# Six separate PSUM banks for the mixing products, weight sums loaded in pieces, and small transfers issued by ScalarE: one change to a fused attention and token-mixing kernel

## The chip, the cores and the metric

The kernel runs on one core of a Trainium2 chip. A core has TensorE (matrix products into PSUM), VectorE, ScalarE and GpSimd (elementwise work), SyncE (which here does nothing but issue transfers) and 16 DMA engines. In the profile they are PE and PEld (matmul and weight load of TensorE), DVE, ACT, POOL and SP. The metric is the device time of one launch in microseconds (us); lower is better.

## What is computed

```python
# attention, per batch and head: only keys of the query's own cluster count
mask = q_assign[:, :, :, None] == k_assign[:, :, None, :]
scores = np.where(mask, scale * np.matmul(q, k.transpose(0, 1, 3, 2)), -1e9)
x = softmax(scores) @ v                      # then laid out as (4, 768, 512)
# token mixing
theta = x @ w_theta
zr, zi = x * np.cos(theta), x * np.sin(theta)
y = np.einsum('ts,bsd->btd', w_tok_r, zr) + np.einsum('ts,bsd->btd', w_tok_i, zi)
u = x + y
out = u + np.maximum(u @ w_ch, 0.0)
```

There are 4 batches of 768 tokens and 512 channels (8 heads of 64). Everything is float32. On TensorE a float32 operand is split into a high and a low part in a shorter float format, and a product is the sum of high by high, high by low and low by high: three matmuls instead of one.

## The kernel before

**Two phases.** The attention of all 16 head pairs comes first (until about 450 us); it writes x to DRAM. The change leaves its code alone. The token mixing of the four batches follows. A batch has six tiles of 128 tokens, numbered n = 6 b + t.

**Per tile: theta.** `theta_parts` (L930) loads the tile's columns of x (`xs`, `load_columns`, L919), splits them (`xh` by ScalarE, L935; `xl` by VectorE in the first two batches, by GpSimd in the last two, L937). `rotation_angle` (L655) makes 12 matmuls into one bank `tp`. `rotation_reduce` (L662) reduces the angle in three VectorE steps (L666 to L668) and takes its absolute value on ScalarE (L670). `rotation_turn` (L651) transposes the tile x on VectorE (`xn` from `xb`, L652) and then issues the next tile's `xb` as four transfers of 64 KB (`load_blocks`, L638, L647); there is one `xb` buffer. Then ScalarE takes two sines (L964; L985 in the first two batches) and VectorE multiplies them by `xn` (L971; L987).

**Batches 0 and 1 ("plain").** `mix` (L1017) multiplies the split tile by the split weights, 48 matmuls, accumulating over the six tiles in six PSUM banks. All six banks are one tile, `y` (L849). After the sixth tile `channel_plain` (L1173) adds y to x (`add_y`, L1152), splits the sum (L1154, L1155) and makes eight groups of 12 matmuls with `w_ch` (L1162), two of them in other banks, six in banks of `y`; `channel_out` (L1166) takes each group out by one VectorE instruction (`ot`, L1169) and one transfer. The order of this stretch is made by a planner that runs the program on a cost model and puts each engine's instructions in the order in which they become ready there.

**Sums of weights.** For batches 2 and 3 the two-by-two block product (cosine and sine parts by the two weights' halves) is made from seven products of sums, as in Strassen's scheme. `make_forms` (L1047) makes the seven split sums of each of six tiles (42 in all: a VectorE sum L1061, a ScalarE cast L1062, a GpSimd subtraction L1063, a store of 384 KB). It is a generator; the plain loop advances it by five steps after each `mix` but the first and the last (L1207). `load_forms` (L1067) loads one tile's seven sums, 384 KB each.

**Batches 2 and 3.** Here the order on each engine, SyncE too, is the program's order (`in_order`, L689). `mix_forms` (L1105) makes 21 matmuls per tile and half of the channels: product m = 4 goes into a bank of its own, `four`, the other six into the six banks of `y`. The first half goes over tiles 0 to 5 while theta of later tiles is worked on, the second half back over 5 to 0. At the end of a half `add_products` (L1116) adds the seven products to x in twelve additions: three instructions of 768 columns for products 4, 3 and 1, and in its second part two of 768 columns that read two banks at once and two of 384. `split_z` (L1079) makes the sums and splits of the rotated tile for the next `mix_forms`; the half of the rotated tile that the second half needs is stored to DRAM (`zd`, L977) and loaded again (`zb`, `load_z`, L1073). `channel` (L1181) starts five groups with the first half's channels and goes on with the second half's.

The sums of tile 4 lie in the buffers `u` of the channel product, those of tile 5 in the place of tile 0's, so neither stays resident: tile 4's seven are loaded between the channel product of one batch and the next batch (L1245, L1295), tile 5's after tile 0's `mix_forms` (L1257), tile 0's again after the second half's tile 5 (L1276). x of the next batch (`load_x`, 1.5 MB) is issued behind the channel product (L1294). All transfers are issued by SyncE, one queue, in order.

Of the kernel before, what the change touches and what calls it, by code (L numbers as in the profile page):

```python
# [9 lines left out]
F32 = mybir.dt.float32  # L10
# [4 lines left out]
ALU = mybir.AluOpType  # L15
AX = mybir.AxisListType
PSUM = bass.MemoryType.PSUM
# [24 lines left out]
def kernel(  # L42
# [19 lines left out]
    nc = tc.nc  # L62
    B, H, D, S = qT.shape
    P = 128
    NP = H // 2
    NT = S // P
    C = cent.shape[0] // H
    DM = w_theta.shape[0]
    NCT = DM // P
    HS = S // 2  # L70
# [4 lines left out]
    xT_d = [dram.tile([P, NP, S], F32, name=f"xT_d{b}") for b in range(B)]  # L75
# [116 lines left out]
    for x in range(3):  # L192
        x = (NPAIR + x) % 3
# [67 lines left out]
    def f(ap):  # L261
        return ap.bitcast(F32)
# [60 lines left out]
    def turn_one_hot(pi, n):  # L323
        ot = bank(f"ot{pi}{n}").bitcast(BF16)[:, 0:S]
        for t in range(NT):
            nc.tensor.transpose(
                out=ot[:, t * P:(t + 1) * P], in_=ohp[:, n, t].rearrange("p j c -> p (j c)"), identity=identb)
        return ot
# [267 lines left out]
    def run(gen):  # L596
        for _ in gen:
            pass
# [39 lines left out]
    def load_blocks(n):  # L638
        if n == B * NT:
            return  # L640
        b, t = divmod(n, NT)
        xb = blocks[n] = ma[0].tile([P, DM], F32, tag="xb", name=f"xb{n}")


        for a in range(P // 32):
            src = xT_d[b][:, :, t * P + 32 * a:t * P + 32 * a + 32]
            nc.sync.dma_start(  # L647
                out=xb[32 * a:32 * a + 32].rearrange("c (n m r) -> c n m r", n=NP, m=P // 32),
                in_=src.rearrange("(m c) n r -> c n m r", c=32))

# [144 lines left out]
    while u <= NUT or todo:  # L795
# [8 lines left out]
        if 0 <= u < NUT:  # L804
            both(score_products, u, exps)
            if u == 0:
# [4 lines left out]
                for n, x in ((1, "mk"), (0, "mq")):  # L811
                    nc.scalar.activation(
                        out=st[1][x], in_=turn_one_hot(1, n), func=AF.Identity,
# [31 lines left out]
    def mpool(name, bufs=1, **kw):  # L845
        return mctx.enter_context(tc.tile_pool(name=name, bufs=bufs, **kw))

    pm = [mpool("pm0", space=PSUM)]
    y = mpool("py", space=PSUM).tile([P, 6, 512], F32, name="y")  # L849
    pm.append(mpool("pm1", space=PSUM))  # L850
    mx = mpool("mx")
    ma.append(mpool("ma1"))
# [12 lines left out]
    def mbank(name):  # L865
        banks[0] += 1
        return pm[(banks[0] - 1) % 2].tile([P, 512], F32, tag="bank", name=name)
# [10 lines left out]
    def load_x(b):  # L878
        xT = xts[b] = mx.tile([P, NP, S], F32, tag="xT", name=f"xT{b}")
        if b == 0:  # L880

            for p in range(NP):
                nc.sync.dma_start(out=xT[:, p], in_=xT_d[b][:, p])
        else:
            nc.sync.dma_start(out=xT, in_=xT_d[b])
# [31 lines left out]
    columns = {}  # L917

    def load_columns(n):  # L919

        b, t = divmod(n, NT)
        if 0 < b < B:
            columns[n] = mxs.tile([P, NCT, P], F32, tag="xs", name=f"xs{n}")
            with tc.issue_after(last_load[0].ins):
                nc.sync.dma_start(out=columns[n], in_=xT_d[b][:, :, t * P:(t + 1) * P])

    PLAIN = 2
    turning = {}
# [31 lines left out]
    z_d = {}  # L960
# [13 lines left out]
    def keep_turned(b, t, rab):  # L974
        zs[b, t] = rab
        z_d[b, t] = dram.tile([P, 2, DM // 2], F32, tag=f"z{t}", name=f"zd{b}_{t}", bufs=2)
        nc.sync.dma_start(out=z_d[b, t], in_=rab[:, :, DM // 2:DM])  # L977

    def rotate(b, t, rab, xn):
        if b < PLAIN:  # L980
# [21 lines left out]

    def y_at(d, c0, c1):
        bank, c = divmod(d * S + c0, 512)
        return y[:, bank, c:c + c1 - c0]

    def cuts(d, c0=0, c1=S):

# [24 lines left out]
    ORDER = (4, 3, 1, 5, 2, 6, 7)  # L1033
    Z_AT = {5: 0, 2: 1, 1: 2, 3: 3, 6: 4, 7: 5, 4: 6}
    Y_AT = {3: 0, 1: 1, 5: 2, 2: 3, 6: 4, 7: 5}
# [28 lines left out]
                nc.sync.dma_start(out=w_f[t][:, m - 1], in_=f(to))  # L1064
                yield

    def load_forms(t):  # L1067
        for m in ORDER:
            nc.sync.dma_start(out=f(forms[t][m]), in_=w_f[t][:, m - 1])

    second = {}
# [28 lines left out]
    four = {}  # L1100

    def product(m):
        return four[0][:, 0:HS] if m == 4 else y[:, Y_AT[m], 0:HS]

    def mix_forms(tiles, first, last):  # L1105

# [9 lines left out]
    def add_products(b, h, k):  # L1116

        x = xts[b][:, 2 * h:2 * h + 2].rearrange("p d (l n) -> p (d l) n", l=2)

        def add(to, of, op):  # L1120
            nc.vector.tensor_tensor(out=to, in0=to, in1=of, op=op)  # L1121

        def twice(m):
            return product(m).unsqueeze(1).broadcast_to([P, 2, HS])

        if k == 0:
            add(x[:, 0:3:2], twice(4), ALU.add)
            add(x[:, 1:4:2], twice(3), ALU.subtract)
            add(x[:, 0:4:3], twice(1), ALU.add)
        else:  # L1130
            add(x[:, 0:4:3], y[:, 2:4, 0:HS], ALU.subtract)
            add(x[:, 1:3], y[:, 2:4, 0:HS], ALU.add)
            add(x[:, 3], product(6), ALU.add)
            add(x[:, 0], product(7), ALU.subtract)

    def split_u_part(b, h, us, eng):

# [7 lines left out]
    def add_y(b, c0, c1):  # L1145

        xT, n = xts[b], c1 - c0
        uh, ul = (u_tile(f"u{x}{b}_{c0}")[:, :, 0:n] for x in "hl")
        for d in range(NCT):
            x = xT[:, d, c0:c1]  # L1150
            for n0, n1, _ in cuts(d, c0, c1):
                nc.vector.tensor_tensor(  # L1152
                    out=xT[:, d, n0:n1], in0=y_at(d, n0, n1), in1=xT[:, d, n0:n1], op=ALU.add)
            nc.scalar.copy(out=uh[:, d, :], in_=x)  # L1154
            nc.gpsimd.tensor_tensor(out=ul[:, d, :], in0=x, in1=f(uh[:, d, :]), op=ALU.subtract)  # L1155
        return uh, ul

    def channel_products(cp, e, u, ds):
        uh, ul = u
        for k, (uu, w) in enumerate(((uh, 0), (uh, 1), (ul, 0))):  # L1160
            for d in ds:
                nc.tensor.matmul(  # L1162
                    cp, lhsT=w_c[d][w][:, e * P:(e + 1) * P], rhs=uu[:, d, :],
                    start=k == 0 and d == 0, stop=k == 2 and d == NCT - 1, skip_group_check=True)
# [8 lines left out]
    def channel_plain(b):  # L1173
        us = [add_y(b, ch * HS, (ch + 1) * HS) for ch in range(2)]
        for x in range(2 * NCT):
            ch, e = divmod(x, NCT)
            cp = (mbank(f"cp{b}_{x}") if x < 2 else y[:, x - 2])[:, 0:HS]
            channel_products(cp, e, us[ch], range(NCT))
            channel_out(b, e, ch, cp)

# [19 lines left out]
    for n in range(PLAIN * NT):  # L1200
        b, t = divmod(n, NT)
        theta(*divmod(n + AHEAD, NT))
        if b == 0:
            weights_after[0] = splits[n + 1]
            next(late_weights, None)
        mix(b, t)
        if 0 < n < PLAIN * NT - 1:  # L1207
            for _ in range(5):
                next(new_forms, None)
        if n == PLAIN * NT - 2:  # L1210
            run(new_forms)
            load_forms(0)
            load_forms(1)
        if t == NT - 1:
            if b == PLAIN - 1:
                load_forms(2)
                load_forms(3)
            channel_plain(b)
            load_x(b + 1)
# [8 lines left out]
    def before(n):  # L1228
        if n < last:
            theta_parts(n, nc.gpsimd)  # L1230
# [10 lines left out]
    def done(n):  # L1241
        if n in turning:
            turned(n)

    load_forms(4)  # L1245
    before(PLAIN * NT + 2)
    z = split_z(PLAIN, 0, 0)
    for b in range(PLAIN, B):
        for t in range(NT - 1):
            n = b * NT + t  # L1250
            done(n + 1)
            angle(n + 2)
            before(n + 3)
            now, z = z, split_z(b, t + 1, 0)
            mix_forms([(t, now)], t == 0, False)
            if t == 0:
                load_forms(5)  # L1257
            turn(n + 2)
            if t == NT - 2:
                load_z(b, 5)  # L1260
        n = b * NT + NT - 1
        load_z(b, 4)
        done(n + 1)
        now, z = z, split_z(b, 5, 1)
        load_z(b, 3)
        mix_forms([(5, now)], False, True)
        angle(n + 2)
        add_products(b, 0, 0)
        now, z = z, split_z(b, 4, 1)
        load_z(b, 2)  # L1270
        add_products(b, 0, 1)
        before(n + 3)
        for t in (5, 4, 3, 2, 1, 0):
            mix_forms([(t, now)], t == 5, t == 0)
            if t == 5:
                load_forms(0)  # L1276
            if t > 1:
                now, z = z, split_z(b, t - 2, 1)
                load_z(b, t - 4)
            else:  # L1280
                now = z
            if t == 5:
                turn(n + 2)
            if t == 4:
                done(n + 2)
                split_u_part(b, 0, us, nc.vector)
        for k in range(2):
            add_products(b, 1, k)
        split_u_part(b, 1, us, nc.vector)
        if b + 1 < B:  # L1290
            z = split_z(b + 1, 0, 0)
        channel(b, us)
        if b + 1 < B:
            load_x(b + 1)  # L1294
            load_forms(4)  # L1295
    in_order(begin)
    mctx.close()

# [50 lines left out]
```

## Time and profile before

| | |
|---|---|
| median of three runs | 886.58 us (885.67 to 886.92) |
| the profiled execution | 885.21 us |
| its span, first to last instruction | 883.4 us |
| TensorE busy | 788.0 us (89%) |
| VectorE, GpSimd, ScalarE busy | 640.4, 563.6, 415.3 us |
| transfers | 135.37 MB, 47.9% of 16 DMA engines |

The durations in the rows below are those of the profiled execution; 1.8 us of its time lie outside the span. A row of the timeline gives the start, the length, engine, line, operation, output and inputs and their shapes, a count, and in brackets the idle time of that engine just before it and what ended that. A row of the waits gives the waiting engine and line, what it waited for, the total in us, the number of times and the longest. A row of the chain gives start, length and what it was. A row of the windows gives from and to, the length, the busy time and number of instructions of each engine, the granted TensorE clock, and the busy share and GB/s of the DMA engines.

### The profile page before, as it was taken

Reading aid. Unit: us, or ns where it says so; the run is one execution under the profiler, and the core shown is the slowest. Engines: PE = TensorE matmul, PEld = TensorE weight load, DVE = VectorE, ACT = ScalarE, POOL = GpSimd, SP = SyncE. Lnnn points to the kernel's source line nnn. Section 1 sums busy time; section 2 is a strip of 40 time slices with the busy share of each in tenths; the row PEclk is TensorE's granted clock in tenths of the full one; section 3 lists DMA queues with packets and bytes.
Section 4 is the critical chain, followed back from the end, with each engine's and each line's share of the span. In section 5 each row is a group of like instructions: output and inputs, shape, how many; then the busy total and the mean of one; then the engine's idle time right before and its main releaser. Section 6 shows DMA issues by size and latency. Waiting matters only on the chain. (4 is left out here: it accounts for less than half of the span.)

```text
span 883.4 us, 14497 instructions
## 1 busy us (share of the span) xinstructions
PE 788.0 (89%) x5316; PEld 576.5 (65%) x5316; DVE 640.4 (72%) x789; ACT 415.3 (47%) x835; POOL 563.6 (64%) x345
## 2 busy tenths in 40 slices
PE   9999999999999999988999955899986878886786
PEld 6656666666666666655567844788765767775675
DVE  7689999999999999976957976745534865237552
ACT  3566666766766666654545444433303332023210
POOL 3677899899999998894739668436603433122420
PEclk9999999999999999998999996999997979898989
DMA  3122333342444433362368665889848452194501
GB/s 127 62 72 65 122 124 119 118 140 84 141 154 152 134 123 115 100 216 95 97 180 235 176 186 189 268 300 329 311 174 287 105 182 75 63 347 91 185 12 72
DMA packets 115234, 135.37 MB, mean 153 GB/s; under 512 B 62226, under 2 KB 81308, under 8 KB 114780
## 3 DMA queue, kind: packets, MB, share of 16 engines
q1 hardware_dynamic: 115164, 134.45, 47.9%
q8 instruction: 42, 0.69, 0.3%
q14 instruction: 28, 0.23, 0.1%
HBM read 96.99 MB, written 37.33 MB: 152 GB/s over the span
## 5 line engine op out<-in xcount | busy, mean ns | idle before, releaser
L485 ACT ACTIVATE at<-sc 128x384 f32<-128x384 f32 x384 | 174.0, 493 | 97.9 <-PE sc L409 51.6
L431 DVE TENSOR_REDUCE nm<-m 128x1 f32<-128x768 f32 x192 | 180.3, 947 | 29.8 <-PE m L409 27.8
L496 POOL TENSOR_TENSOR acc<-at,at 128x768 f32<-128x768 f32 x64 | 125.9, 1967 | 40.1 <-ACT at L485 40.1
L409 PE MATMUL m<-hk,hq 64*128 64x384 f32 x384 | 147.6, 385 | 0.2 <-DVE nm L431 0.2
L557 PE MATMUL av<-at,vt 128*64 128x384 f32 x768 | 145.7, 500 | 0.2 <-ACT xt L572 0.2
L496 POOL TENSOR_TENSOR acc<-acc,at 128x768 f32<-128x768 f32 x64 | 132.9, 2076 | 10.8 <-ACT at L485 8.7
L409 PE MATMUL m<-mk,mq 64*128 64x384 f32 x384 | 128.5, 335 | 0.1
L409 PE MATMUL sc<-hq,hk 64*128 64x384 f32 x384 | 117.2, 392 | 6.6 <-ACT at L485 6.4
L409 PEld LDWEIGHTS sc<-hq,hk 64*128 64x128 f32 x384 | 55.4, 184 | 69.2 <-issue 25.3
L409 PE MATMUL sc<-hq,lk 64*128 64x384 f32 x384 | 97.4, 336 | 0.0
L409 PE MATMUL sc<-mq,mk 64*128 64x384 f32 x384 | 97.3, 336 | 0.0
L409 PE MATMUL sc<-lq,hk 64*128 64x384 f32 x384 | 97.0, 335 | 0.0
L557 PEld LDWEIGHTS av<-at,vt 128*64 128x64 f32 x768 | 46.6, 136 | 59.1 <-issue 54.1
L1097 POOL TENSOR_TENSOR zf<-zt,zf 128x384 fp32r<-128x384 f32 x24 | 24.8, 1031 | 82.1 <-ACT zf L1096 82.1
L409 PEld LDWEIGHTS m<-hk,hq 64*128 64x128 f32 x384 | 70.7, 184 | 2.0 <-DVE nm L431 1.4
L409 PEld LDWEIGHTS m<-mk,mq 64*128 64x128 f32 x384 | 71.4, 186 | 0.8 <-DVE mk L374 0.4
L500 DVE TENSOR_TENSOR acc<-acc,acc 128x768 f32<-128x768 f32 x30 | 63.5, 2117 | 0.0
L1063 POOL TENSOR_TENSOR ws<-sum,ws 128x384 fp32r<-128x384 f32 x30 | 35.2, 1178 | 33.2 <-ACT ws L1062 33.2
L409 PEld LDWEIGHTS sc<-mq,mk 64*128 64x128 f32 x384 | 54.6, 185 | 0.0
L409 PEld LDWEIGHTS sc<-lq,hk 64*128 64x128 f32 x384 | 54.5, 186 | 0.0
L409 PEld LDWEIGHTS sc<-hq,lk 64*128 64x128 f32 x384 | 54.4, 185 | 0.0
L1024 PE MATMUL y<-wr_hi,z 128*128 128x512 f32 (+1 forms) x192 | 49.9, 341 | 4.1 <-DVE ot L1169 2.5
(222 smaller groups left out, 1775.2 us busy)
## 6 DMA issues: line engine op xcount, KB each, us to landing
wf<-ws SPq DMA_DIRECT2D x42, 384.0 KB
ws<-wf SPq DMA_DIRECT2D x20, 384.0 KB
vt<-in_v_dram SPq DMA_DIRECT2D x16, 384.0 KB
rb<-sd SPq DMA_DIRECT2D x32, 192.0 KB
xT_d<-xt SPq DMA_DIRECT2D x16, 384.0 KB
xb<-xT_d SPq DMA_DIRECT2D x96, 64.0 KB
out_dram<-ot SPq DMA_DIRECT2D x32, 192.0 KB
rawq<-in_qT_dram SPq DMA_DIRECT2D x15, 384.0 KB
```

What stands on the lines that cost most here:

```text
L409: nc.tensor.matmul(out, lhsT=stat[r, cols], rhs=mov[r, over], start=start, stop=stop)
L431: nc.vector.tensor_reduce(out=s["nm", a][:, j, i // 2:i // 2 + 1], in_=s["m", j][:, :, 0:HS], op=ALU.max, axis=AX.XY, negate=True)
L485: last_exp[0] = nc.scalar.activation(out=s["at", a, i][:, j], in_=s["sc", j], func=AF.Exp, scale=SCALE)
L496: last_acc[0] = nc.gpsimd.tensor_tensor(out=s["acc", a, x], in0=prev, in1=at, op=ALU.add)
L500: nc.vector.tensor_tensor(out=s["acc", a, 0], in0=s["acc", a, 0], in1=s["acc", a, 1], op=ALU.add)
L557: nc.tensor.matmul(s["av"][64 * j:64 * j + 64], lhsT=s["vt"][:, i, j, :], rhs=s["at", a, i][:, j], start=(i == 0), stop=(i == NT - 1))
L1024: last_mix[0] = nc.tensor.matmul(y_at(d, c0, c1), lhsT=zz[:, d * P:(d + 1) * P], rhs=ww[:, c0:c1], start=first and lead, stop=last, skip_g ...
L1063: nc.gpsimd.tensor_tensor(out=lo, in0=src, in1=f(hi), op=ALU.subtract)
L1097: nc.gpsimd.tensor_tensor(out=l_, in0=of, in1=f(h_), op=ALU.subtract)
```

## The change

- The one tile `y` of six banks becomes six tiles of one bank. The second part of `add_products` becomes six additions of 384 columns, each of one product.
- `load_forms` can load some of the seven sums: the first four, then the other three. Tile 4's come after `mix_forms` of tiles 0 and 1 of the same batch, tile 5's after tiles 2 and 3, tile 0's after the second half's tiles 5 and 4.
- x of batch 3 is loaded after tile 2 of batch 3, and no longer right behind the channel product of batch 2. That of batch 2 stays where it was.
- The `xb` transfers from n = 2 on, all `xs` and all `zd` are issued by ScalarE's queue. What is issued for xb stands behind the transpose (L652) and ahead of the sines.
- `make_forms` is not advanced after the last `mix` of a batch; in batch 1 it is advanced by six steps where it was five.

```diff
-            nc.sync.dma_start(
+            (nc.sync if n < 2 else nc.scalar).dma_start(
                 out=xb[32 * a:32 * a + 32].rearrange("c (n m r) -> c n m r", n=NP, m=P // 32),
...
-    y = mpool("py", space=PSUM).tile([P, 6, 512], F32, name="y")
+    py = mpool("py", space=PSUM)
+    y = [py.tile([P, 512], F32, name=f"y{x}") for x in range(6)]
...
-                nc.sync.dma_start(out=columns[n], in_=xT_d[b][:, :, t * P:(t + 1) * P])
+                nc.scalar.dma_start(out=columns[n], in_=xT_d[b][:, :, t * P:(t + 1) * P])
...
-        nc.sync.dma_start(out=z_d[b, t], in_=rab[:, :, DM // 2:DM])
+        nc.scalar.dma_start(out=z_d[b, t], in_=rab[:, :, DM // 2:DM])
...
-    def load_forms(t):
-        for m in ORDER:
+    def load_forms(t, ms=ORDER):
+        for m in ms:
             nc.sync.dma_start(out=f(forms[t][m]), in_=w_f[t][:, m - 1])
...
-            add(x[:, 0:4:3], y[:, 2:4, 0:HS], ALU.subtract)
-            add(x[:, 1:3], y[:, 2:4, 0:HS], ALU.add)
-            add(x[:, 3], product(6), ALU.add)
-            add(x[:, 0], product(7), ALU.subtract)
+            for m, less, more in ((5, 0, 1), (2, 3, 2), (6, None, 3), (7, 0, None)):
+                if less is not None:
+                    add(x[:, less], product(m), ALU.subtract)
+                if more is not None:
+                    add(x[:, more], product(m), ALU.add)
...
-        if 0 < n < PLAIN * NT - 1:
-            for _ in range(5):
+        if 0 < n < PLAIN * NT - 1 and t < NT - 1:
+            for _ in range(5 if b == 0 else 6):
                 next(new_forms, None)
...
-    load_forms(4)
     before(PLAIN * NT + 2)
...
-            if t == 0:
-                load_forms(5)
+            if t < 4:
+                load_forms(*((4, ORDER[:4]), (4, ORDER[4:]), (5, ORDER[:4]), (5, ORDER[4:]))[t])
+            if t == 2 and b > PLAIN:
+                load_x(b)
...
             if t == 5:
-                load_forms(0)
+                load_forms(0, ORDER[:4])
+            if t == 4:
+                load_forms(0, ORDER[4:])
...
         channel(b, us)
-        if b + 1 < B:
-            load_x(b + 1)
-            load_forms(4)
```

More of the change, by code (lines that the diff above doesn't have):

```diff
@@ L1004, in y_at @@
         bank, c = divmod(d * S + c0, 512)
-        return y[:, bank, c:c + c1 - c0]
+        return y[bank][:, c:c + c1 - c0]
     def cuts(d, c0=0, c1=S):
@@ L1102, in product @@
     def product(m):
-        return four[0][:, 0:HS] if m == 4 else y[:, Y_AT[m], 0:HS]
+        return four[0][:, 0:HS] if m == 4 else y[Y_AT[m]][:, 0:HS]
     def mix_forms(tiles, first, last):
@@ L1176, in channel_plain @@
             ch, e = divmod(x, NCT)
-            cp = (mbank(f"cp{b}_{x}") if x < 2 else y[:, x - 2])[:, 0:HS]
+            cp = (mbank(f"cp{b}_{x}") if x < 2 else y[x - 2])[:, 0:HS]
             channel_products(cp, e, us[ch], range(NCT))
```

## The prediction

> **What bounds the kernel now.** I read the page, then the windows by stage, the waits of the mixing phase, the chain, and the timelines around each idle stretch of TensorE. The attention phase is not touched, so all that counts lies behind 455 us.
>
> ```profile
> 521.67:539.06 17.39, 0.01 (x1) 0.00 (x0) 12.06 (x17) 9.00 (x17) 11.26 (x9) 0.65 0.64 202
> ...
> 576.05:634.00 57.95, 56.29 (x313) 48.61 (x313) 28.11 (x39) 20.43 (x38) 29.30 (x26) 1.00 0.93 311
> ...
> 660.40:709.00 48.60, 36.10 (x172) 32.05 (x173) 30.02 (x38) 17.01 (x30) 18.47 (x15) 0.89 0.66 195
> ...
> 773.00:822.00 49.00, 37.14 (x175) 32.81 (x173) 26.24 (x44) 14.74 (x26) 14.33 (x13) 0.90 0.66 208
> ```
>
> The busy times are those of PE, PEld, DVE, ACT and POOL; then come the granted clock, the DMA share and GB/s. Batch 1's mixing (576 to 634) is TensorE at work 97% of the time: there TensorE is the bound, and what delays it before comes out at the end. The stretch at 522 is TensorE standing still. In the first halves of batches 2 and 3 (660 to 709, 773 to 822) TensorE works only three quarters of the time at a clock of 0.89 and 0.90: there something else ends last. The waits say what:
>
> ```profile
> PE cp L1162 <- ACT uh L1154: 19.3, 3, 17.4
> ...
> PE y L1162 <- DVE ot L1169: 12.1, 17, 1.0
> ...
> PE tp L659 <- ACT xh L935: 12.0, 2, 8.6
> DVE zt L1087 <- DMA zb<-zd: 10.4, 3, 4.2
> ...
> PE tp L659 <- DVE rab L667: 7.9, 3, 5.9
> ...
> PE y L1024 <- DVE ot L1169: 2.5, 1, 2.5
> ```
>
> Four causes on TensorE: a channel product that waits for its input in batch 0 (17.4), matmuls into `y` that wait for VectorE's reads of `y`, theta that waits for its columns, and theta that waits for VectorE.
>
> **Part 1: six banks as six tiles.** The chain within a channel product:
>
> ```profile
> 756.88 1.04 PE four L1162 x6
> ...
> 759.00 0.57 DVE ot L1169
> ...
> 759.61 1.34 PE y L1162 x6
> ...
> 760.98 0.57 DVE ot L1169
> ```
>
> TensorE and VectorE alternate. The group at 759.61 writes another bank than the one that the `ot` at 759.00 read, and still starts when that read is over; groups in `four` have no such wait. So the dependence goes by tile. With one tile per bank no group waits for its neighbour's `ot`: the 12.1 and 2.5 go, **14.6 us**. What is late next is VectorE's `ot` itself, 0.57 beside groups of 1.04: it keeps up.
>
> The same at the ends of the halves:
>
> ```profile
> 699.69 3.31 PE L1112 MATMUL y<-u,zf 128*128 128x384 f32 x18
> ...
> 716.88 2.74 DVE L1121 TENSOR_TENSOR xT<-xT,y 128x768 f32<-128x768 f32 x4
> ...
> 719.68 3.25 PE L1112 MATMUL y<-ws,zf 128*128 128x384 f32 x9 [2.92 <-DVE xT L1121]
> ...
> 725.31 0.70 PE L1112 MATMUL four<-u,zf 128*128 128x384 f32 x3
> 744.96 4.72 DVE L1121 TENSOR_TENSOR xT<-xT,y 128x768 f32<-128x768 f32 x6 [2.19 <-PE y L1112]
> ...
> 749.74 1.01 PE L1162 MATMUL y<-u,wch_hi 128*128 128x384 f32 x2 [3.77 <-DVE xT L1121]
> ...
> 827.67 3.24 PE L1112 MATMUL y<-ws,zf 128*128 128x384 f32 x9 [3.51 <-DVE xT L1121]
> ...
> 832.31 0.68 PE L1112 MATMUL four<-u,zf 128*128 128x384 f32 x3
> ```
>
> Between the halves, the 18 matmuls wait for the last of the additions and then take 5.6 us (719.68 to 725.31) where 3.31 is their usual time: after the idle stretch they run slowly. With single banks each product follows its own addition, and TensorE ends one product (3 of 18, 0.55 us) behind VectorE, not 5.7: 5.1 less in batch 2; in batch 3 the 18 take 4.6 (827.67 to 832.31): 4.1 less. In the second part of the additions two instructions of 768 columns become four of 384. Two double ones are worth 4.72 - 2.74 = 1.98, which leaves 0.38 for each single one in the 2.74, so four for two is a gain of 0.5 at that price and as much lost where a short one takes over half of a long one; I take 0.3 lost, since an instruction has a fixed part. That makes 4.8 and 3.8. At the channel product, the additions of products 4, 3 and 1 run while TensorE still makes the others. The 24 matmuls from 749.74 last until 756.88; now they start at 749.74 - 3.77 = 745.97 and run at the speed of the row at 756.88 (six in 1.04, 24 in 4.2): 6.7 earlier, of which I take 6.5, in two batches 13. VectorE and ScalarE then have the second half's split done about when TensorE asks for it; this has a few tenths to spare, and if it has not, 1 to 2 of the 13 stay. Sum of these places: **21.6 us**.
>
> **Part 2: sums in pieces, another queue.** What stands ahead of theta in batches 2 and 3:
>
> ```profile
> 775.04 7.67 DMA u<-wf
> ...
> 782.77 7.70 DMA ws<-wf
> ...
> 792.05 5.58 DMA xb<-xT_d
> ...
> 672.44 2.07 PE L659 MATMUL tp<-wth_hi,xh 128*128 128x512 f32 x4 [8.64 <-ACT xh L935]
> ...
> 708.86 1.09 PE L659 MATMUL tp<-wth_hi,xh 128*128 128x512 f32 x4
> ...
> 714.39 0.71 PE L1112 MATMUL four<-ws,zf 128*128 128x384 f32 x2 [2.60 <-DVE xT L1121]
> ```
>
> The chain passes through two sets of seven sums before four transfers of 64 KB get their turn: small transfers stand in SyncE's order behind 14 loads of 384 KB. After the change tile 4's and 5's sums come in four portions, one per tile of about 8 us, and are used at tile 4 and 5, so they hide behind `mix_forms`. Gone with it: in batch 2 the 8.64 and the slow start behind it (2.07 for four matmuls against 1.09; about 2 for a whole theta, an estimate); in batch 3 the rest of the waits for `xh` and most of those for `rab` (12.0 - 8.6 = 3.4, and 5.9), with 3 for two slow starts; and the 2.60 at 714.39, because `zb` no longer stands behind `xb` on SyncE (VectorE waits up to 4.2 for it ahead of the additions, by the waits above). That is 10.6 + 12.3 + 2.6, **25.5 us**. What SyncE's loads are moved past: `zb` and the output's transfers, which stay in its order. x of batch 3 moves from ahead of tile 0 to tile 2 and is wanted only at the additions, four tiles later: nothing.
>
> A rule of the Trainium skill speaks against this part: DMA: Bandwidth & Descriptors, section "Issuing engines are not separate DMA queues", says that transfers issued by different engines run on the same 16 DMA engines and interleave, so that a second issuer saves issue time alone. Before the change one queue issues everything, so no row here can show it; by that rule the transfers would still wait behind the sums in the engines, and what that would cost is worked out as rival 2.
>
> **Part 3: what ScalarE pays.** No row shows an issue by ScalarE. SyncE's rows, and the loop of a tile:
>
> ```profile
> 698.68 2.63 SPq L647 DMA_DIRECT2D xb<-xT_d  x4
> 701.35 0.64 SPq L977 DMA_DIRECT2D zd<-rab  x1
> 702.03 0.62 SPq L925 DMA_DIRECT2D xs<-xT_d  x1
> ```
> ```profile
> 699.44 1.31 DVE L971 TENSOR_TENSOR rab<-rab,xn 128x512 f32<-128x512 f32 x2 [0.79 <-ACT rab L964]
> 700.86 1.38 DVE L1087 TENSOR_TENSOR zt<-rab 128x256 f32<-128x256 f32 x1
> ...
> 705.87 0.70 DVE L652 STREAM_TRANSPOSE xn<-xb 128x512 f32<-128x512 f32 x1
> 707.65 1.30 DVE L971 TENSOR_TENSOR rab<-rab,xn 128x512 f32<-128x512 f32 x2 [1.08 <-ACT rab L964]
> ...
> 706.99 0.63 ACT L964 ACTIVATE rab<-rab 128x512 f32<-128x512 f32 x1
> ...
> 716.01 0.42 DVE L1087 TENSOR_TENSOR zt<-zb 128x256 f32<-128x256 f32 x1
> ```
>
> From one multiplication (L971) to the next a tile takes 8.2 us, longer than TensorE's work for it; the loop goes through VectorE and ScalarE. The four `xb` issues now wait for the transpose (over at 706.57) on ScalarE, and the sines are queued behind them, and VectorE's L971 behind the sines. At SyncE's 2.63 the first sine would start at 709.2, not 706.99: 2.2 later. If an issue costs ScalarE nothing, it is 0. Some comes back: `zd` and `xs` (1.26) push GpSimd's `xl` later, out of the way of `zt`, which takes 1.38 beside GpSimd and 0.42 without. I take 1.3 a tile, nearer to the row of 2.63, the only price shown, in eight tiles: 10. In the second half of batch 2 the same issues stand ahead of `zf`: 1.5. In batches 0 and 1 twelve tiles pay up to 3.25 (39 in all) or nothing; ScalarE is busy 20.43 of 57.95 us there, and theta runs two tiles ahead, so I take 4. Sum: **15.5 us lost**, between 0 and 60.
>
> **Part 4: no sums in front of a channel product.** VectorE while TensorE stands still in batch 0:
>
> ```profile
> 530.00 0.56 DVE L1061 TENSOR_TENSOR sum<-ws,ws 128x384 f32<-128x384 f32 x1 [2.61 <-DMA ws<-wd2r]
> ...
> 536.66 1.33 DVE L1061 TENSOR_TENSOR sum<-ws 128x384 f32<-128x384 f32 x1
> 537.92 0.87 DVE L1152 TENSOR_TENSOR xT<-y,xT 128x384 f32<-128x384 f32 x2
> ```
>
> The additions that the channel product waits for come last (537.92). If only the sum at 536.66 goes, 1.3 is won; if none of the stretch is left but what batch 1 has, 15.5 (17.4 less the 1.9 of the other two waits). The wait of 2.61, the two sums and some single ones make about 5.5, and single banks let the first additions start before the last tile's mixing is over. But which sums are the five steps left out, the rows do not say, and the planner orders anew. I take **7 us**. The steps move into batch 1's mixing, one more per tile, hidden by TensorE (VectorE busy 28.11, GpSimd 29.30 of 57.95); without that cover a sum is about 1 us.
>
> **Sum.** 14.6 + 21.6 + 25.5 + 7 - 15.5 = 53.2. The profiled execution, 885.2 (span 883.4 and 1.8 around it), becomes 832; the median of the runs is 1.4 above it, so **833 us**.
>
> **Rivals.** (1) An issue costs ScalarE next to nothing: the 15.5 stay, 818. For it: nothing but that ScalarE is idle half of the time. (2) The small transfers gain nothing by the other queue while 16 engines carry the sums (the DMA share is 0.93 in batch 1): an xb landing would keep the 5.58 it has at 792.05 and half of part 2's 25.5 stays out, 846. Against it: sums come in portions. The Trainium skill's rule named in part 2 is this case. (3) The banks don't separate, by a dependence that still covers all six: 14.6 + 21.6 come back, 869. Against it: `four`, a tile of its own, shows no such wait. (4) Slower: ScalarE's queue becomes the bound. It gets 22 x 4 + 18 + 12 = 118 issues; at 0.63 each that is 74 us. If all of it lies on the path, in the plain stretch too, where sines and casts queue behind issues that wait for the transpose, 74 takes the place of 15.5: 892. It decides from 69 us on, 0.58 for every issue. Against it: ScalarE's 20.43 of 57.95.
>
> **How the numbers follow.** Forecast 0.53, rival 1 0.15, rival 2 0.18, rival 3 0.07, rival 4 0.05, something else 0.02. The range, 814 to 862, takes in the forecast with part 4's bounds (825 to 839), rivals 1 and 2, and losses at ScalarE of up to 44 in place of 15.5; left out are rivals 3 and 4. Faster by over 0.2% (1.8 us, about what a measurement of this kernel can tell from no change) 0.94, within 0.01, slower 0.05.
>
> **What would show it.** Right: no wait of `y` for `ot` (L1169) or for L1121 over 1 us; the last `y` product of a half about 0.6 us behind the last addition; the chain between the batches free of `u<-wf`; L971 to L971 about 9.5 us in batch 2; the stretch before batch 0's channel product about 10 us. Wrong: waits for `xs` or `xb` of several us in batches 2 and 3 (rival 2), ScalarE's four issues well under 1 us (rival 1), or TensorE below 90% in batch 1's mixing with ScalarE named (rival 4).

## The result and the profile after

| | before | after |
|---|---|---|
| median of three runs, us | 886.58 (885.67 to 886.92) | 860.01 (856.19 to 860.90) |
| ratio | | 0.9691, 95% interval 0.9645 to 0.9738 |
| span of the profiled execution | 883.4 | 858.2 |
| end of batch 0's mixing | 521.7 | 526.6 |
| start of channel product 2 | 744.8 | 743.9 |
| channel product 2 | 28.2 | 16.8 |
| from its end to channel product 3 (batch 3's tiles) | 78.3 | 76.8 |
| channel product 3 | 28.0 | 16.8 |

Faster by 26.6 us, half of the 53.2 forecast. By the places in the table, 22.6 of the 25.2 us by which the span shrank come from two short stretches, the channel products of batches 2 and 3. Up to the first of these the kernel is only 0.9 us ahead, and that hides two larger changes: channel product 1 ends 13.5 earlier (646.2 for 659.7, in the table of places below), and batch 2's tiles, from there to channel product 2, take 12.6 longer (97.7 for 85.1). Batch 3's tiles give 1.5. The windows of after, the columns as before:

```profile
526.56:533.97 7.41, 0.03 (x1) 0.00 (x0) 4.66 (x7) 3.47 (x8) 6.61 (x6) 0.85 0.74 211
561.70:623.20 61.50, 61.50 (x338) 53.06 (x337) 34.94 (x55) 25.54 (x46) 31.24 (x26) 1.00 0.94 307
655.50:703.90 48.40, 34.66 (x154) 30.09 (x154) 22.45 (x39) 13.37 (x24) 13.35 (x11) 0.83 0.65 209
...
743.90:760.70 16.80, 16.80 (x98) 16.80 (x97) 9.39 (x18) 3.13 (x5) 3.50 (x3) 1.00 0.25 87
760.70:806.60 45.90, 33.21 (x154) 29.50 (x152) 22.47 (x40) 13.62 (x24) 12.38 (x11) 0.85 0.64 208
```

The stretch ahead of batch 0's channel product is 7.41 us where it was 17.39. Batch 1's mixing has TensorE at work without a break. The channel product (743.90 to 760.70) is 98 matmuls in 16.80 us with no idle time at a clock of 1.00; before, the same 98 took 28.20 with 21.08 busy at 0.88. The first halves of batches 2 and 3 are no better than before: TensorE works 72% of the time (34.66 of 48.40, 33.21 of 45.90). The waits of the mixing phase, after:

```profile
DVE rab L972 <- ACT rab L965: 34.5, 10, 8.8
...
DVE ot L1171 <- DMA out_dram<-ot: 20.0, 9, 5.4
...
ACT rab L965 <- DMA xb<-xT_d: 15.0, 5, 3.9
DVE xn L652 <- DMA xb<-xT_d: 14.7, 4, 8.7
...
PE tp L659 <- ACT xh L936: 10.6, 1, 10.6
...
ACT rab L965 <- DMA ws<-wf: 8.0, 1, 8.0
...
PE y L1113 <- DMA ws<-wf: 8.0, 1, 8.0
```

No row of TensorE waiting for `ot` is left, and its wait for the additions (L1122) is 0.5 in all. In their place stand the sines (L965), which wait for the `xb` issues ahead of them in ScalarE's order, the multiplications (L972), which wait for the sines, theta, which once waits 10.6 for the cast of its columns, and products that wait for sums of weights. One tile's loop in batch 2:

```profile
676.47 0.63 ACT L670 ACTIVATE rab<-rab 128x512 f32<-128x512 f32 x1 [4.13 <-DVE rab L668]
677.09 2.66 ACTq L647 DMA_DIRECT2D xb<-xT_d  x4
679.79 0.63 ACT L965 ACTIVATE rab<-rab 128x512 f32<-128x512 f32 x1 [2.69 <-DMA xb<-xT_d]
```
```profile
680.46 1.31 DVE L972 TENSOR_TENSOR rab<-rab,xn 128x512 f32<-128x512 f32 x2 [3.40 <-ACT rab L965]
689.71 1.31 DVE L972 TENSOR_TENSOR rab<-rab,xn 128x512 f32<-128x512 f32 x2 [3.40 <-ACT rab L965]
```

Four issues take ScalarE 2.66 us, which is SyncE's price of before (2.63), and VectorE idles 3.40 for the sine; from one L972 to the next it is 9.25. The start of batch 2, and that of batch 3 with the queues of SyncE and ScalarE:

```profile
655.46 1.33 PE L1113 MATMUL four<-ws,zf 128*128 128x384 f32 x3 [6.50 <-DMA ws<-wf]
665.71 2.67 PE L1113 MATMUL y<-ws,zf 128*128 128x384 f32 x6 [7.96 <-DMA ws<-wf]
```
```profile
761.73 3.39 SPq L1070 DMA_DIRECT2D u<-wf  x7
765.22 3.80 SPq L1070 DMA_DIRECT2D ws<-wf  x4
770.60 0.32 SPq L886 DMA_DIRECT2D xT<-xT_d  x1
```
```profile
767.44 6.94 ACTq L647 DMA_DIRECT2D xb<-xT_d  x4
774.43 0.63 ACT L965 ACTIVATE rab<-rab 128x512 f32<-128x512 f32 x1 [8.02 <-DMA ws<-wf]
...
782.81 0.59 ACTq L926 DMA_DIRECT2D xs<-xT_d  x1
783.50 0.62 ACT L936 CAST xh<-xs 128x512 fp32r<-128x512 f32 x1 [7.83 <-DMA zd<-rab]
```
```profile
784.17 2.08 PE L659 MATMUL tp<-wth_hi,xh 128*128 128x512 f32 x4 [10.64 <-ACT xh L936]
```

In batch 3 the portions of the sums, meant one per tile, go out in one run: eleven loads of 384 KB from 761.73 to 769.02, and the 1.5 MB of x behind them. ScalarE's four issues of 64 KB, in the middle of this, take 6.94 from the first to the last instead of 2.66, though each is short.

What holds them is in the row of 774.43: landings of sums (`ws`, loads on SyncE's queue), which pass no data to `xb` or to the sines. The trace shows how. The landing of a transfer is told by a semaphore, a counter that an engine can wait for. The program has eight for the transfers of both queues, each used by 77 or 78 transfers in turn, and an issue waits until the last transfer on its semaphore has landed. The second, third and fourth of these issues start at 769.63, 771.58 and 773.82, each 0.03 behind the landing of a load of sums. It goes on behind them: the `xb` issued at 769.63 takes 13.1 to land, where about 2.5 is usual in batch 2's loop, and the next issue of columns (`xs`) waits for its semaphore until 782.74. The cast at 783.50 stands behind that issue in ScalarE's order, though the columns that it takes were issued at 750.45 already, and theta stands still for 10.64.

### The profile page after: what moved, and what is told of

It is laid out like the page before. It is cut to its first block, busy times and chain, and to the rows that moved or that the text cites. A ratio compares the mean times of both kernels' runs of the same rounds, so it can differ in the third digit from the quotient of the medians.

```text
span 858.2 us, 14512 instructions
## 1 busy us (share of the span) xinstructions
PE 785.1 (91%) x5316; PEld 578.1 (67%) x5316; DVE 635.1 (74%) x797; ACT 415.0 (48%) x835; POOL 564.2 (66%) x345
## 5 line engine op out<-in xcount | busy, mean ns | idle before, releaser
L485 ACT ACTIVATE at<-sc 128x384 f32<-128x384 f32 x384 | 173.8, 493 | 100.4 <-PE m L409 53.2
L431 DVE TENSOR_REDUCE nm<-m 128x1 f32<-128x768 f32 x192 | 180.4, 947 | 29.9 <-PE m L409 23.9
L496 POOL TENSOR_TENSOR acc<-acc,at 128x768 f32<-128x768 f32 x64 | 131.8, 2059 | 13.4 <-ACT at L485 11.4
```

The lines of the kernel that those rows point to most:

```text
L431: nc.vector.tensor_reduce(out=s["nm", a][:, j, i // 2:i // 2 + 1], in_=s["m", j][:, :, 0:HS], op=ALU.max, axis=AX.XY, negate=True)
L485: last_exp[0] = nc.scalar.activation(out=s["at", a, i][:, j], in_=s["sc", j], func=AF.Exp, scale=SCALE)
L496: last_acc[0] = nc.gpsimd.tensor_tensor(out=s["acc", a, x], in0=prev, in1=at, op=ALU.add)
```

## The experiments

The theory after this comparison: banks and portions bring most of what was forecast, and ScalarE's queue takes half of it away, by its place in ScalarE's order and because SyncE loses what paced it. The rivals: the portions work only together with the second queue; the moved steps of the sums make the sums late; a second queue's transfers land late whatever issues them. A letter in an expectation names a theory of that expectation alone. The kernels were measured in three groups, each beside runs of the kernel before, with medians of 885.59 (banks, all by SyncE, sums' steps, queue), 884.51 (the first exchange of places, `xb`, `xs` and `zd`, sines) and 886.08 (the other two exchanges and the two kernels with portions).

The places in time, from the timelines of the profiled executions (us):

| kernel | end of batch 0's mixing | channel 1 ends | channel 2 | batch 3's tiles | channel 3 ends |
|---|---|---|---|---|---|
| before | 521.7 | 659.7 | 744.8 to 773.0 | 78.3 | 879.3 |
| queue alone | 525.9 | 666.3 | 742.4 to 769.5 | 80.9 | 878.5 |
| portions alone | 521.0 | 662.3 | 738.4 to 765.6 | 70.4 | 864.0 |
| banks alone | 521.9 | 642.8 | 738.6 to 755.4 | 77.7 | 849.9 |
| banks and portions | 520.3 | 639.7 | 729.8 to 746.6 | 65.9 | 829.3 |
| after, all by SyncE | 520.9 | 638.7 | 728.4 to 745.2 | 67.0 | 829.0 |
| after | 526.6 | 646.2 | 743.9 to 760.7 | 76.8 | 854.3 |
| after, `xb` by SyncE | 520.0 | 641.2 | 726.5 to 743.3 | 64.2 | 824.3 |
| after, `xs`, `zd` by SyncE | 526.1 | 647.7 | 742.5 to 759.3 | 71.7 | 847.9 |
| after, sines first | 525.6 | 645.8 | 733.8 to 750.6 | 76.2 | 843.6 |

**Banks alone.** The kernel before with six single banks and the additions that go with them.

```diff
-    y = mpool("py", space=PSUM).tile([P, 6, 512], F32, name="y")
+    py = mpool("py", space=PSUM)
+    y = [py.tile([P, 512], F32, name=f"y{x}") for x in range(6)]
...
```

> The kernel before with the six single banks alone (and the additions of one product each). By the forecast's own sum this part is worth 14.6 + 21.6 = 36 us, which gives 850 us. Theory A (the other parts lose what is missing from the forecast) expects 846 to 856 and no wait of a y product for ot or for the additions. Theory B (the banks' gain itself is lost, because what waits behind the channel products in batches 2 and 3 is set by loads that come no earlier) expects 862 to 875, with the waits for xs and xb ahead of theta grown by what the channel products gave.

Measured: 855.68 (854.12 to 856.00), ratio 0.9663 (0.9635 to 0.9690). Of its waits of TensorE:

```profile
PE cp L1164 <- ACT uh L1156: 10.7, 1, 10.7
PE y L1113 <- DMA ws<-wf: 9.7, 2, 9.1
...
PE four L1113 <- DMA ws<-wf: 1.7, 1, 1.7
```

The banks alone bring 29.9, no less than the whole change (the two intervals overlap) and at the slow end of what was expected of them. Both channel products are 16.8 long. The wait ahead of batch 0's channel product falls from 17.39 to 10.7 without a step of the sums moved. And a new wait comes up, 10.8 at the start of batch 2, for sums that aren't there yet: the banks bring it, not the queue and not the moved steps.

**The changed kernel with all transfers on SyncE.**

```diff
-            (nc.sync if n < 2 else nc.scalar).dma_start(
+            nc.sync.dma_start(
                 out=xb[32 * a:32 * a + 32].rearrange("c (n m r) -> c n m r", n=NP, m=P // 32),
...
-                nc.scalar.dma_start(out=columns[n], in_=xT_d[b][:, :, t * P:(t + 1) * P])
+                nc.sync.dma_start(out=columns[n], in_=xT_d[b][:, :, t * P:(t + 1) * P])
...
-        nc.scalar.dma_start(out=z_d[b, t], in_=rab[:, :, DM // 2:DM])
+        nc.sync.dma_start(out=z_d[b, t], in_=rab[:, :, DM // 2:DM])
```

> The changed kernel with all small transfers back on SyncE's queue; banks, pieces and the sums' steps stay. Theory Q (ScalarE's issues are what was missed: they hold ScalarE up in batches 0 and 1, make the last sums of weights late, and lengthen the tile loop of batches 2 and 3 to 9.5 us) expects it faster than the changed kernel, 838 to 852, with the tile loop back at 8.0 us, batch 0's mixing over by 522 and no wait of the first products of batch 2 for their sums. Theory P (the steps moved out of the front of the channel products make the last sums late, and the loads, which nothing paces, hold up the small transfers) expects the 14 us of waits for the sums to stay, and waits for xs ahead of theta in batch 3: 858 to 872.

Measured: 834.72 (833.17 to 835.05), ratio 0.9428 (0.9405 to 0.9450). The queue costs the changed kernel 25.3, more than the prediction's 15.5. That is faster than either theory expected. Theory Q's shorter loop is there, but not the end of the waits for sums: 13.2 are left at the start of batch 2. Two multiplications of batch 2, and SyncE's order at the start of batch 3:

```profile
668.38 1.31 DVE L972 TENSOR_TENSOR rab<-rab,xn 128x512 f32<-128x512 f32 x2 [0.75 <-ACT rab L965]
...
676.22 1.30 DVE L972 TENSOR_TENSOR rab<-rab,xn 128x512 f32<-128x512 f32 x2 [0.79 <-ACT rab L965]
```
```profile
746.86 1.98 SPq L1070 DMA_DIRECT2D u<-wf  x4
750.82 2.63 SPq L647 DMA_DIRECT2D xb<-xT_d  x4
753.55 2.07 SPq L978 DMA_DIRECT2D zd<-rab  x1
755.72 0.59 SPq L926 DMA_DIRECT2D xs<-xT_d  x1
756.40 1.55 SPq L1070 DMA_DIRECT2D u<-wf  x3
```

The loop is 7.84 long and VectorE waits 0.79 for the sine. On SyncE the small transfers, which wait for the tile's work, stand between the portions and so pace them: the next three loads go out at 756.40, a tile after the first four. No wait of theta for its columns is left in batches 2 and 3.

**The sums' steps as before.** The changed kernel, its queue kept, with five steps after every `mix` but the first and last.

```diff
-        if 0 < n < PLAIN * NT - 1 and t < NT - 1:
-            for _ in range(5 if b == 0 else 6):
+        if 0 < n < PLAIN * NT - 1:
+            for _ in range(5):
```

> The changed kernel with the steps of the sums of weights where they were before (five after every mixing, the last tile's too). Theory P expects the wait of batch 2's first products for their sums (6.5 and 8.0 us in the changed kernel) gone or down to 3, and batch 0's channel product to wait longer than the 7.4 us of the changed kernel, up to 17: together 848 to 862. Theory Q expects the wait for the sums to stay at 10 or more, and 860 to 870.

Measured: 857.85 (854.77 to 861.04), ratio 0.9693 (0.9659 to 0.9727), the same as after within the intervals.

```profile
PE y L1113 <- DMA ws<-wf: 7.6, 1, 7.6
PE cp L1164 <- ACT uh L1156: 7.4, 1, 7.4
PE four L1113 <- DMA ws<-wf: 6.3, 1, 6.3
```

The time lies in theory P's range, but neither of its signs came: the wait ahead of batch 0's channel product is 7.4 with the steps moved or not, and the wait for sums stays too. Where the steps stand in the program makes no difference; that the planner orders them anew would account for it.

**Queue alone.** The kernel before with `xb` from n = 2 on, `xs` and `zd` on ScalarE's queue (the reverse of the second diff above, on the kernel before).

> The kernel before with the small transfers on ScalarE's queue alone. If the queue helps by itself (the forecast gave it, with the pieces, 25.5 us and a cost of 15.5), 870 to 884. Theory Q expects it slower than before, 888 to 905, since the issues cost ScalarE in every tile and the loads still stand in the same bursts. Theory P expects 876 to 890: the waits for xs (8.6 ahead of batch 2) go, the tile loop grows by 1.5 us.

Measured: 884.19 (882.62 to 887.19), ratio 0.9991 (0.9974 to 1.0009): no change.

```profile
PE cp L1162 <- ACT uh L1154: 17.5, 3, 15.5
PE y L1162 <- DVE ot L1169: 15.8, 17, 2.8
PE tp L659 <- ACT xh L935: 11.7, 2, 9.9
```

Theory P's range takes this in, theory Q's (888 to 905) does not. With the sums still loaded whole, theta waits 11.7 for the cast of its columns where it waited 12.0. In batch 2 the cast comes earlier (the longest wait of before, 8.6, is gone there), in batch 3 later: 9.9. There the same happens as in after: the four `xb` issues take 6.57 because they wait for landings of sums, their transfers take 6.7 to 10.1 to land, and the issue of `xs` and the cast wait behind one of them. So the ratio of 1 is a balance and not a queue without effect. By the table of places 6.6 are lost up to the end of channel product 1, 9.0 won in batch 2's tiles (76.1 for 85.1), and 2.6 lost in batch 3's. How much of the 9.0 is only that batch 2 starts later was not tried.

**Tile 0's sums in another place.** The changed kernel on SyncE, with the resident places of tile 0's and tile 1's sums exchanged. Tile 0's lay in the four buffers in which the sums are made, so they couldn't be loaded before the last sum was.

```diff
-    PLACE = {0: (24, 25, 26, 27, 0, 1, 2), 1: range(3, 10), 2: range(10, 17), 3: range(17, 24)}
+    PLACE = {0: range(3, 10), 1: (24, 25, 26, 27, 0, 1, 2), 2: range(10, 17), 3: range(17, 24)}
```

> The changed kernel with the small transfers on SyncE (834.7), and the resident places of tile 0's and tile 1's sums exchanged: tile 0's seven sums no longer go into the four buffers in which the sums are made. Theory L (the 13 us that batch 2's first products wait come from the place: tile 0's sums can't be loaded before all 42 are made): the wait for sums ahead of batch 2 falls from 13.1 us to under 4, 822 to 829. Rival M (the making of the sums is late as a whole, and tile 1's or theta's inputs are late next): the wait moves to tile 1 or to theta at much the same size, 832 to 837.

Measured: 829.64 (829.12 to 831.49), ratio 0.9388 (0.9360 to 0.9416). The wait for sums (13.2 in the kernel that it starts from) is gone from the waits of TensorE, and another has come up:

```profile
PE y L1113 <- DVE ot L1171: 7.1, 4, 4.5
```

So the place did make the products wait for sums, but over half of that time is kept by the next wait, for VectorE to take channel product 1's outputs out of the same banks. The time lies between the two theories. The intervals just overlap, so the 5 us are likely and not sure. The same exchange in two other kernels says to count on less.

In the kernel of the next paragraph (`xb` by SyncE):

> The changed kernel with xb back on SyncE (830.8) and the resident places of tile 0's and tile 1's sums exchanged. Theory L: of the 10.2 us that batch 2's first products wait for sums some 4 to 6 are won, as in the kernel with all small transfers on SyncE (834.7 to 829.6): 824 to 828. Rival M (another wait takes their place whole): 829 to 832.

Measured: 831.07 (830.00 to 831.89), ratio 0.9379 (0.9352 to 0.9405), against 830.78 without the exchange: nothing. The wait for `ot` is 9.7 there, the waits for sums were 10.2.

In the changed kernel itself:

> The changed kernel with the resident places of tile 0's and tile 1's sums exchanged, ScalarE's queue kept. Theory L: the 14.5 us of waits for sums ahead of batch 2 go for the most part, and other waits give half of it back: 850 to 856. Rival M: theta's columns by ScalarE's queue are as late, 857 to 862.

Measured: 856.89 (854.76 to 857.59), ratio 0.9669 (0.9637 to 0.9700), against 860.01: not to be told from after. 14.5 of waits for sums went, 12.0 for `ot` came, and theta's wait for the cast of its columns is no shorter than in after (11.9 for 10.6). The time lies between the two theories: that another wait takes the place is shown, but it is mostly the one for `ot`, which neither had named.

**Which transfers cost.** The changed kernel with `xb` alone back on SyncE (the first line of the second diff):

> The changed kernel with xb alone back on SyncE; xs and zd stay with ScalarE. Theory Q (the cost is the four xb issues ahead of the sines in ScalarE's order): multiplication to multiplication in batch 2 falls from 9.5 to about 8.0 us, 836 to 843. Rival T (two queues that share the engines: whatever goes by the second queue lands late): xs and zd still pay, 846 to 856.

Measured: 830.78 (829.77 to 831.87), ratio 0.9401 (0.9369 to 0.9433).

And the other way round, `xs` and `zd` back on SyncE, `xb` left with ScalarE (the other two lines):

> The changed kernel with xs and zd back on SyncE; xb stays with ScalarE. Theory Q: the loop of a tile stays at 9.2 to 9.9 us, 852 to 860. Rival T: xs lands early again, theta waits less for xh, 840 to 850.

Measured: 854.29 (853.62 to 854.71), ratio 0.9662 (0.9635 to 0.9690).

```profile
676.02 1.31 DVE L972 TENSOR_TENSOR rab<-rab,xn 128x512 f32<-128x512 f32 x2 [3.40 <-ACT rab L965]
686.44 1.31 DVE L972 TENSOR_TENSOR rab<-rab,xn 128x512 f32<-128x512 f32 x2 [3.39 <-ACT rab L965]
```
```profile
769.69 0.53 SPq L978 DMA_DIRECT2D zd<-rab  x1
770.31 0.57 SPq L926 DMA_DIRECT2D xs<-xT_d  x1
770.98 1.54 SPq L1070 DMA_DIRECT2D u<-wf  x3
```

The four `xb` issues per tile are the cost: back on SyncE they bring 29.2, more than either theory expected, the two others 5.7, where the intervals of this ratio and of after's overlap. In the second kernel the loop is still 10.4, with the same 3.40 ahead of the multiplication. But `zd` on SyncE paces the portions again (770.98, one tile behind the first four at 761.02), and batch 3's tiles take 71.7 instead of 76.8. `xs` and `zd` by ScalarE do no harm by themselves (830.78 with them there, 834.72 with all by SyncE), so rival T's numbers miss. Its reason, that transfers by the second queue land late, does hold for `xb` in the changed kernel's batch 3: 9.3 to 13.1 from issue to landing.

**The sines first.** The changed kernel with the next tile's `xb` issued behind the two sines, in batches 2 and 3.

```diff
-        rotation_turn(n, xn)
+        nc.vector.transpose(out=xn, in_=blocks.pop(n))
+        if n < PLAIN * NT + 2:
+            load_blocks(n + 1)
...
             sines(turning[n][4])
+            load_blocks(n + 1)
```

> The changed kernel with the two sines ahead of the next tile's xb issues in ScalarE's order, in batches 2 and 3. Theory Q: multiplication to multiplication in batch 2 about 8.0 to 8.6 us; batches 0 and 1 and the late sums keep their share, 843 to 852. Rival T (the transfer, not the place of its issue): xb lands as late as before or later, 857 to 864.

Measured: 847.50 (846.64 to 849.39), ratio 0.9589 (0.9560 to 0.9619). Multiplications and theta:

```profile
678.58 1.30 DVE L974 TENSOR_TENSOR rab<-rab,xn 128x512 f32<-128x512 f32 x2 [0.74 <-ACT rab L967]
686.17 1.87 DVE L974 TENSOR_TENSOR rab<-rab,xn 128x512 f32<-128x512 f32 x2 [0.79 <-ACT rab L967]
692.63 2.96 DVE L974 TENSOR_TENSOR rab<-rab,xn 128x512 f32<-128x512 f32 x2 [0.79 <-ACT rab L967]
```
```profile
775.15 2.08 PE L659 MATMUL tp<-wth_hi,xh 128*128 128x512 f32 x4 [11.67 <-ACT xh L936]
```

The same transfers by the same queue, two places later in ScalarE's order: the loop is 7.6 and 6.5 instead of 9.25 to 9.9, batch 2 ends 10.1 earlier, and 12.5 are won. So two fifths to a half of the queue's 25 is ScalarE's order (12.5 by the medians of two groups of runs, 10.6 by the spans of the profiled executions). The 11.67 at the start of batch 3 stay: nothing paces SyncE here either, and the issue of `xs` at 773.79 again waits for the landing of an `xb`, which takes 14.2. Batch 0's mixing ends as late (525.6).

**Portions alone, and with the banks.** The kernel before with the sums' loads as in the change, everything by SyncE and one tile for the banks:

```diff
...
-            if t == 0:
-                load_forms(5)
+            if t < 4:
+                load_forms(*((4, ORDER[:4]), (4, ORDER[4:]), (5, ORDER[:4]), (5, ORDER[4:]))[t])
+            if t == 2 and b > PLAIN:
+                load_x(b)
...
```

> The kernel before with the sums' loads in pieces alone: one tile for the six banks, SyncE for all transfers, the sums' steps as before. Theory P (the prediction's part 2: the chain past 14 whole loads is a cost of its own, 25.5 us, whatever the banks and queue): 857 to 865. Rival B (part of it hides behind the waits for banks, or the portions need the second queue): 870 to 882.

Measured: 867.75 (866.27 to 869.84), ratio 0.9797 (0.9764 to 0.9830): 18.3, between the two theories. Theta waits for its columns in neither batch; but the waits for banks take some of it, as rival B has it: those for `ot` are 15.3 (12.1 before) and those of `y` for the additions at the halves 7.6 (6.4 before).

Banks and portions, without queue and without moved steps:

> The kernel before with six single banks and the sums' loads in pieces; SyncE for all transfers, the sums' steps as before. If the steps' place makes no difference here either, 833 to 837, as with the steps moved (834.7). If leaving out the steps ahead of a channel product is worth the 7 us that the prediction gave it, 840 to 844.

Measured: 834.28 (830.97 to 837.36), ratio 0.9417 (0.9381 to 0.9452). That is the changed kernel on SyncE (834.72, steps moved): the moved steps are worth nothing. Banks and portions together bring 51.8, more than the 29.9 and 18.3 that they bring alone.

## Why the prediction came out half right

The sign and the directions of parts 1 to 3 held, and 860 lies inside the range; the size is off by 26.6, from three terms: banks and portions 9.9 short, the sums' steps 7, the queue 9.8.

| part | forecast | measured |
|---|---|---|
| 1, banks | +36.2 | +29.9 alone |
| 2, portions | +25.5 | +18.3 alone; 1 and 2 together +51.8, not 61.7 |
| 3, ScalarE's issues | -15.5 | -25.3 in the changed kernel |
| 4, sums' steps | +7 | 0 |

**Part 1: right, with one wait not seen.** The dependence goes by tile, as was read from the `four` rows: with single banks no product waits for a neighbour's `ot`, and the additions hold TensorE 0.5 in all in after. The two channel products give 22.6; the prediction's terms there were 13 for their start and, of the 12.1 for `ot`, the 3.3 in each of them, 19.6 together. By the table of places the banks alone give 16.9 up to the end of channel product 1, lose 10.7 in batch 2's tiles and give 22.6 in channel products 2 and 3. What the sum lacked is the wait of batch 2's first products for their sums: 10.8 with the banks alone, 14.5 after, none before. It is the "what is late next" that the prediction asked for elsewhere and not here. In the kernel before, the last cast of a sum ends at 630.8 and batch 2's first product starts at 644.6; in after the last cast ends at 655.7. Shown is that every kernel with single banks has either this wait or, with the places exchanged, a wait of 7 to 12 us for `ot` in its place, and that the kernels without them have neither for long (0.7 at most). Why the planner puts the last sums later there was not tried.

**Part 2: the portions right, the second queue not needed.** Batch 3's tiles go from 78.3 to 70.4 alone and from 77.7 to 65.9 beside the banks; 12.3 were forecast there. Batch 2's tiles go from 85.1 to 76.1 alone and from 95.8 to 90.1 beside the banks, where the wait for sums has come up; 13.2 were forecast. The part took "sums in pieces, another queue" as one step; the runs take it apart: portions alone 18.3, queue alone nothing in sum (0.9991), as a balance of 9.0 won in batch 2's tiles and about as much lost before and after. Beside banks and portions the queue only costs: all by SyncE the same kernel is 25.3 faster. Rival 2 was half right: transfers by the second queue did land late in batch 3, `xb` after 9.3 to 13.1 where the rival kept 5.58, but in batch 2's loop they landed after about 2.5. The wait of 10.6 is in batch 3 only. The prediction set a rule of the Trainium skill against this part (DMA: Bandwidth & Descriptors, "Issuing engines are not separate DMA queues": a second issuer saves only issue time). The ratio of 0.9991 alone does not decide on it, because ScalarE's losses are in it too.

**Part 3: the price of an issue right, its consequences undersized.** The step that failed is "I take 1.3 a tile ... in eight tiles: 10", with 4 for the plain batches. An issue costs ScalarE 0.65, as on SyncE, and a tile 1.4 to 2.0 (9.25 to 9.87 against 7.84 to 8.0 on SyncE). But batch 0's mixing ends 5.7 later, and the portions lost their pace: the prediction named what SyncE's loads are moved past, and not that the transfers taken out of SyncE's order were what held the loads back. It also put at nothing that an issue by ScalarE can wait for the landing of SyncE's loads: at the start of batch 3 ScalarE stands 5.5 at the four `xb` issues and 4.0 at the `xs` issue until a landing frees their semaphores. No run gives the two queues semaphores of their own, so what this costs by itself stays open. Stage by stage after loses to the same kernel on SyncE 7.5 up to the end of channel product 1, 8.0 in batch 2's tiles and 9.8 in batch 3's: 25.3. What the 7.5 of the first two batches consist of was not taken apart. Rival 1 (an issue costs nothing) is excluded by the 2.66; rival 4 by batch 1's mixing, where TensorE is busy 61.50 of 61.50.

**Part 4: the forecast stretch, by another cause.** "About 10 us" was forecast and 7.41 found, but banks alone give 10.7. The rest goes with batch 0's mixing ending 5.7 later, and is no gain: in all kernels with single banks whose mixing ends by 522 the stretch is 9.6 to 11.5 long, in those where it ends at 525.6 or later 7.3 to 8.5. That VectorE and ScalarE catch up meanwhile is the likely reason. The five steps left out are worth nothing in either pair of kernels (857.85 and 860.01; 834.28 and 834.72).

**What to do with it.** The changed kernel with `xb` on SyncE is 29 us faster than the change (830.78 against 860.01) and 54 faster than before (884.51 in its group). All by SyncE with the places exchanged (829.64), and both together (831.07), are no different from it within the intervals.

## What to carry to other kernels

Before moving a transfer to a computing engine's queue, look at what stands behind it in that engine's order, and put it behind the work that others wait for; in the changed kernel four issues of 0.65 ahead of the sines cost more than the queue could win. Look also at what the issue itself waits for: where the queues share the semaphores that tell of landings, an engine that issues small transfers waits for the other queue's bulk loads. A transfer that waits for work is also a brake on the bulk loads behind it in the same queue: take it out, and portions meant one per tile go out in one run. And when a wait is removed, the next one has to be looked for at the place where the engine arrives earlier, not only at the place that was freed.

## What the runs showed of the hardware

An issue mostly costs ScalarE 0.65, but it can stand still there for longer. All 84 `xb` issues of the mixing phase, after:

```profile
L647 ACTq DMA_DIRECT2D xb<-xT_d x84: 564/647/5817, 459.4 to 795.0; - x84
```

The three numbers are the shortest, the median and the longest in ns. The longest held ScalarE for 5.8 us in batch 1 (573.76 to 579.58, with a DMA share of 0.98); no wait for a semaphore ends in it, and what held it the rows don't say. The four at 767.44 are each short: the 6.94 over which they are spread are waits between them, for landings of other transfers, as told above. On SyncE such a wait holds up other transfers; on ScalarE it holds up the sines and casts behind it.

TensorE's clock went with its rest. Channel product 2 before, in the columns of the windows:

```profile
744.80:773.00 28.20, 21.08 (x98) 19.19 (x97) 11.26 (x18) 3.11 (x5) 3.50 (x3) 0.88 0.14 49
```

With 7.1 us idle among them 98 matmuls ran at a granted 0.88 and kept TensorE busy for 21.08; without a wait they ran at 1.00 in 16.80 (the row of 743.90 above). Of the 11.4 us won there 7.1 are waits, and 4.3 is the faster running of the same matmuls: a wait taken out of a dense row of matmuls was worth more than its own length.
